# Storing the first 1664 rows of dw2 from GpSimd's queue by row number, eight of 128 partitions apart

## The chip, the cores and the metric

The kernel runs on one core of one Trainium2 chip. The core has five engines with a queue of instructions each: PE (TensorE, matrix multiply), DVE (VectorE), ACT (ScalarE), POOL (GpSimd) and SP (SyncE, here only for issuing transfers). Transfers between the chip's memory (DRAM) and the on-chip memory (SBUF, 128 partitions) can be issued by SP, ACT and POOL; sixteen transfer engines carry them out. A transfer adds 16 to its semaphore when it has landed, one for each transfer engine. The metric is the device time of one execution in microseconds (us), the median of the runs.

## The reference

What is computed is one backward step of a gated mix of two blocks, for one token: attention over a cache (32 heads, 4096 keys of 128) and a dense block with the mish activation (640 to 1728 to 640).

```python
def _fwd_reference(A_x, A_k_cache, A_v_cache, A_wq, A_wo, B_x, B_w1, B_b1, B_w2, gate_w):
    ...
    x = A_x
    g = _sigmoid((x * gate_w).sum(-1, keepdims=True))
    a = _A_ref(x, A_k_cache, A_v_cache, A_wq, A_wo)
    b = _B_ref(x, B_w1, B_b1, B_w2)
    return g * a + (1 - g) * b
...
    _out, _vjp = jax.vjp(_f, A_x, A_k_cache, A_v_cache, A_wq, A_wo, B_w1, B_b1, B_w2, gate_w)
    _grads = _vjp(grad_out)
    return (_out0, *[jnp.asarray(_g) for _g in _grads])
```

The outputs are the forward result and the gradients of all inputs but B_x. The gradients of the two caches have the size of the caches, 32 MB each; they are outer products of one row of numbers with one column per head. The gradient of w2, called dw2 here, is an outer product too: row f of its 1728 rows is the activation of f times one common row of 640 numbers.

## The kernel before

All in all 82 MB are read and 82 MB written. The kernel goes once over the 32 heads (loop variable h; `H - 1` rounds and a last one written out after the loop). For each head it loads K and V, transposes them in words of two bf16 on PE into PSUM (L515), copies them from there to SBUF with ACT (L524), multiplies them with q and with the gradient of the output (L538), takes the softmax and its backward step, makes the two outer products dv and dk on DVE (L598, two halves each) and stores them from SP (L616). Between these it works off two side jobs: the projections wq and wo in groups of four heads (g, `hh = h % 4`), and the dense block, cut into small steps in a list `mq`, of which each round takes some.

The order on every engine is the order of the program's text (a schedule by hand); an instruction waits for what it needs, and what stands behind it on its queue waits with it. SP's transfers use eight semaphores in turn, so an SP issue also waits until the transfer eight issues before has landed.

What matters here:

- `w2_sb` holds w2 in SBUF as 128 partitions of 13 rows of 640 (1664 rows), and the last 64 rows as a fourteenth slice on 64 partitions. Row `p * 13 + fc` of w2 stands on partition p in slice fc, so that each partition's 13 rows are 16,640 bytes in one piece in DRAM.
- When the dense block's sums are done, `m_dw2(fc)` (L501 to L503, ACT) writes slice fc of dw2 over slice fc of `w2_sb`. `dw2_some` takes the next one or two of them in a round, counted by `dw2_next`.
- In round `h == H - 4`, that is head 28 (L796 to L802), dw2 is stored: three pieces of the 1664 rows from SP (L799; slices 0 to 3, 4 to 7 and 8 to 12), the last 64 rows and the gradient of b1 from POOL (L800, L802). POOL has nothing else to do then and reaches its stores long before SP comes to head 28.
- In the same round, after the stores, ACT makes dwo of the group before with four instructions (`f_dwo`, L380), and SP stores it (L386).
- In round `h == H - 2` dw1 is stored (L805, L806).
- After the loop come the last head, the last group's wq and wo (L372, L383) with their stores, and the three small results, `fin_rows`, stored from POOL (L920 to L922). L948 stands for the closing instructions of the program.
- `dx_parts` is a float tile of which DVE fills one column per group; it is used from the second group on.
- `ident_bf` is the 128 x 128 identity, made by POOL at the start (L159, L160).

Of the kernel before, what the change touches and what calls it, by code (L numbers as in the profile page):

```python
# [8 lines left out]
ALU = mybir.AluOpType  # L9
AX = mybir.AxisListType  # L10
# [6 lines left out]
def kernel(  # L17
# [24 lines left out]
    nc = tc.nc  # L42
    P = 128
    _, H, Sk, Dh = A_k_cache.shape
# [8 lines left out]
    FR = F // P  # L53
    FM = FR * P
# [4 lines left out]
    W2P = [(0, 4), (4, 8), (8, FR)]  # L59
# [17 lines left out]
    dw2_v = out_8[0:FM, :].rearrange("(p fc) n -> p fc n", p=P)  # L77
# [11 lines left out]
    const = ctx.enter_context(tc.tile_pool(name="const", bufs=1))  # L89
# [59 lines left out]
    w2_sb = const.tile([P, FCN, D], BF16, name="w2_sb")  # L149
    for a, b in W2P:  # L150
# [7 lines left out]
    ident_bf = const.tile([P, P], BF16, name="ident_bf")  # L158
    nc.gpsimd.memset(ident_bf[:], 0.0)  # L159
    nc.gpsimd.affine_select(  # L160
        out=ident_bf[:], in_=ident_bf[:], compare_op=ALU.not_equal, fill=1.0,
        base=0, pattern=[[-1, P]], channel_multiplier=1,
# [20 lines left out]
    nc.vector.memset(aT_acc[:], 0.0)  # L183
    bT = const.tile([P, RC], F32, name="bT")
    dx_parts = const.tile([P, RC, NG + 3], F32, name="dx_parts")

    p4b, ds4b = [], []
    qz = const.tile([P, G, 2, 2, 16], BF16, name="qz")
# [57 lines left out]
    def g_qpair_cp(g):  # L246
        pair_cp(qz, groups[g].pop("pair"), 4)

    def g_docol(g):
        groups[g]["col"] = col_mm(groups[g]["do_row"])  # L250
# [163 lines left out]
    def m_np(fc):  # L414
        return P if fc < FR else FT
# [60 lines left out]
    def m_diag():  # L476
        nc.vector.tensor_copy(dh_bf[:, 0:FR], dh32[:, 0:FR])
        nc.vector.tensor_copy(dh_bf[0:FT, FR:FCN], dh32[0:FT, FR:FCN])
        nc.gpsimd.tensor_tensor(diag3, ident_bf[:].unsqueeze(2).to_broadcast([P, P, FR]),
                                dh_bf[:, 0:FR].unsqueeze(1).to_broadcast([P, P, FR]), ALU.mult)  # L480
        nc.gpsimd.tensor_tensor(mjunk[0:FT, FM:F], ident_bf[0:FT, 0:FT],
                                dh_bf[0:FT, FR:FCN].to_broadcast([FT, FT]), ALU.mult)
# [18 lines left out]
    def m_dw2(fc):  # L501
        n = m_np(fc)
        nc.scalar.activation(w2_sb[0:n, fc, :], db_bc[0:n, :], ACT.Copy, scale=act_f[0:n, fc:fc + 1])  # L503
# [14 lines left out]
    def ev():  # L518
        trq.pop(0)()
# [6 lines left out]
    def k_pe(h, c):  # L526
        if h < H:
            tr_pe(h, kts, KT, c)

    def v_pe(h, c):  # L530
        if h < H:
            tr_pe(h, vts, VT, c)
# [32 lines left out]
    def softmax(h):  # L565
        mx = s_ps.tile([P, P + 2], F32, name="mx", tag="mx")
        nc.tensor.transpose(mx[:, 0:P], dgms.pop(h)[:].to_broadcast([P, P]), ident_f[:])  # L567
        negM = small.tile([P, 1], F32, name="negM", tag="negM")
        nc.vector.tensor_reduce(negM[:], mx[:, 0:P], axis=AX.X, op=ALU.max, negate=True)  # L569
        return mx, negM  # L570

    def exps(h, negM):
        es[h] = small.tile([P, J], BF16, name="e_bf", tag="e_bf")
        zds[h] = small.tile([P, 2], F32, name="zd", tag="zd")
        nc.scalar.activation(es[h][:], sd[h][0], ACT.Exp, bias=negM[:], scale=scale, accum_out=zds[h][:, 0:1])  # L575
# [21 lines left out]
    def outer(dst, col4, row, a, b):  # L597
        nc.vector.tensor_tensor(  # L598
            dst[:, a:b, :].rearrange("p j (k t) -> p j k t", t=4),
            row.rearrange("p (k t) -> p k t", t=4).unsqueeze(1).to_broadcast([P, b - a, Dh // 4, 4]),  # L600
            col4[:, a:b, :].unsqueeze(2).to_broadcast([P, b - a, Dh // 4, 4]), ALU.mult)

    o_t = {}

    def out_half(w, h, dst, col4, row, k):
        hh = h % G
        if k == 0:
            if w == "k" and H - KBUFS <= h < H - 1:
                o_t[w, h] = kv_in.tile([P, J, Dh], BF16, name="Kn", tag="Kn")
            elif w == "v" and h > H - VBUFS:  # L610
                o_t[w, h] = kv_in.tile([P, J, Dh], BF16, name="Vn", tag="Vn", bufs=VBUFS)
            else:
                o_t[w, h] = outs.tile([P, J, Dh], BF16, name="o_sb", tag="o_sb")
        outer(o_t[w, h], col4, row[:, hh * Dh:(hh + 1) * Dh], k * JH, (k + 1) * JH)
        if k == 1:
            nc.sync.dma_start(dst[h], o_t.pop((w, h))[:])  # L616

    def dv_out(h, k):
        out_half("v", h, dVv, p4s[h], groups[h // G]["do_row"], k)
# [1 line left out]
    def dk_out(h, k):  # L621
        if h >= 0:
            out_half("k", h, dKv, ds4s[h], groups[h // G]["qs_row"], k)
# [12 lines left out]
    def dqo_red(h, x):  # L636
        if h >= 0:
            v = x[:].rearrange("p t r -> p (t r)")[:, 3:3 + 4 * (P - 1)].rearrange("p (s q) -> p s q", q=P - 1)
            nc.vector.tensor_reduce(groups[h // G]["dqo"][:, :, h % G],  # L639
                                    v[:, :, 0:P - 1:32].rearrange("p s (i c) -> p i s c", i=2),  # L640
                                    axis=AX.XY, op=ALU.add)
# [6 lines left out]
    m_cost = dict(h=0.8, b1=0.8, act=0.9, b=0.5, dh=0.9, diag=0.5, bc=0.5, dx=0.9, dw1=0.5, gap=0.0)  # L648
    m_fn = dict(h=m_h, b1=lambda i: (m_b1(), m_abs()), act=m_act, b=m_b, dh=m_dh,
                diag=lambda i: m_diag(), bc=m_bc, dx=m_dx, dw1=m_dw1)  # L650
    dw2_next = [0]

    def mlp_some(budget, pause=True):
        spent = 0.0
# [88 lines left out]
    for h in range(H - 1):  # L743
        g, hh = h // G, h % G
        nx, pv = g + 1 < NG, g > 0
        k_pe(h + 1, 2)
        ev()
        mx, negM = softmax(h)
        if hh == 3 and nx:
            g_qpair_cp(g + 1)  # L750
            g_docol(g + 1)
        dqo_red(h - 1, xs[h])
        k_pe(h + 1, 3)
        ev()
        exps(h, negM)
        dk_out(h - 1, 1)
        v_pe(h + 1, 0)
        if hh == 2 and nx:
            g_q(g + 1)
        v_pe(h + 1, 1)  # L760
        if hh == 3 and nx:
            g_dopair(g + 1)
            g_dopair_cp(g + 1)
        k_rows(h + 1)
        ev()
        ev()
        pjs(h)
        v_pe(h + 1, 2)
        ev()
        zd_mm(h, mx)  # L770
        if hh == 0 and pv:
            f_new(g - 1)
            f_diag(g - 1)
        elif h >= 2:
            mlp_some(0.9, False)
        v_pe(h + 1, 3)
        ev()
        probs(h, mx)
        if hh == 0 and pv:
            f_o4(g - 1)  # L780
            f_o4c(g - 1)
            f_bc(g - 1)
        dv_out(h, 0)
        k_pe(h + 2, 0)
        dq_o(h)
        v_rows(h + 1)
        rw_cp(h + 1)
        if h + 2 < H:
            ev()
        dv_out(h, 1)  # L790
        load_k(h + KBUFS)
        load_v(h + VBUFS)
        k_pe(h + 2, 1)
        if h + 2 < H:
            ev()
        if h == H - 4:  # L796
            assert dw2_next[0] == FCN
            for a, b in W2P:
                nc.sync.dma_start(dw2_v[:, a:b, :], w2_sb[:, a:b, :])  # L799
            nc.gpsimd.dma_start(out_8[FM:F, :], w2_sb[0:FT, FR, :])  # L800
            assert not any(k == "bc" for k, _ in mq)
            nc.gpsimd.dma_start(db1_row, dh_bc[0:1, :])  # L802
        if h == H - 2:
            assert not mq
            nc.sync.dma_start(dw1_v[:, 0:3, :], w1_sb[:, 0:3, :])  # L805
            nc.sync.dma_start(dw1_v[:, 3:RC, :], w1_sb[:, 3:RC, :])  # L806
        dk_out(h, 0)
        x_tr(h + 1)
        maxes(h + 1)
        if hh == 0:  # L810
            if nx:
                g_new(g + 1)
            if pv:
                l_pe(g - 1, 0, G)
                l_add(g - 1, g - 1, True)
                for t in range(G):
                    f_dwo(g - 1, t)
                f_dwo_st(g - 1)
                for c in range(2):
                    f_dx(g - 1, c)  # L820
                    f_dwq(g - 1, c)
        if hh == 1:
            if pv:
                for c in range(2, RC):
                    f_dx(g - 1, c)
                    f_dwq(g - 1, c)
                f_dwq_st(g - 1)
            if nx:
                w_pe("o", g + 1, 0)
                ev()  # L830
                w_pe("o", g + 1, 1)
                ev()
        if hh == 2:
            if g + 2 < NG:
                load_wo(g + 2)
            if not nx:
                for k in range(NWT):
                    w_pe("q", g, k)
                    ev()
            else:  # L840
                w_pe("o", g + 1, 2)
                ev()
                g_do(g + 1)
                g_qcol(g + 1)
                g_qpair(g + 1)
        if hh == 3:
            if g % 2 == 0 and g + 4 <= NG:
                load_wqp(g // 2 + 1)
            if nx:
                g_qs(g + 1)  # L850
        if h >= 2:
            mlp_some(0.9 if hh < 2 else 1.8)
            dw2_some(2)

    g, h = NG - 1, H - 1
# [97 lines left out]
```

## Time and profile before

| | us |
|---|---|
| median of 3 runs | 404.71 |
| lowest and highest of them | 404.71 to 405.26 |
| the profiled execution | 404.96 |
| its span, from the first instruction to the last | 403.18 |
| PE busy in the span | 305.9 |
| DVE busy | 287.9 |
| ACT busy | 232.4 |
| POOL busy | 11.8 |
| DRAM read and written, mean rate | 82.03 and 82.03 MB, 407 GB/s |

The page divides the span into 40 slices of 10.1 us; a digit is the busy share of an engine in that slice in tenths. Transfers are counted by queue: q1 is what SP issues, q0 what POOL issues, q8 and q14 fetch instructions. A group of instructions is named by its line, its engine, its operation and what it writes and reads. The windows view gives the busy time of each engine in chosen stretches, and behind it the granted clock of TensorE, the share of the sixteen transfer engines that was busy, and what they moved. The chain of waits is followed back from the last instruction, at each step to what released it. The sixteen increments of a transfer are read from the trace's record of semaphore updates by transfers.

### The profile page before, as it was taken

How to read it: one execution, taken by the hardware profiler on the slowest of the kernel's cores; microseconds unless marked ns; L12 is line 12 of the kernel's file. 1: busy time of each engine (PE TensorE's matmuls, PEld its weight loads, DVE VectorE, ACT ScalarE, POOL GpSimd, SP SyncE). 2: the span in 40 equal slices, each digit the busy share in tenths (PEclk: the TensorE clock that was granted, in tenths of full speed). 3: DMA queues.
4: the chain of work that ended last, by engine and by line, in shares of the span. 5: the costliest groups of instructions: out<-in, count | busy, mean ns of one | idle time of the engine just before them, and what ended most of it. 6: DMA issues, size and time to landing. Idle time of an engine off the chain costs nothing.

```text
span 403.2 us, 7688 instructions
## 1 busy us (share of the span) xinstructions
PE 305.9 (76%) x2930; PEld 207.0 (51%) x2945; DVE 287.9 (71%) x808; ACT 232.4 (58%) x468; POOL 11.8 (3%) x29
## 2 busy tenths in 40 slices
PE   2979989787897985876887779876886977677640
PEld 1556646464565663544555447544555645464420
DVE  2217738868678875769897956896997985679780
ACT  2466757754676563753668667765767655375220
POOL 3000001000000000000001200000000000000001
PEclk9999999988999998989998997988999899889555
DMA  7999999999999999999999999999999999999894
GB/s 274 428 416 423 417 424 415 417 423 424 422 422 426 423 414 424 424 418 428 422 423 428 424 418 424 427 418 423 422 419 424 425 417 425 426 422 377 360 389 153
DMA packets 28708, 164.55 MB, mean 408 GB/s; under 512 B 2991, under 2 KB 3056, under 8 KB 12288
## 3 DMA queue, kind: packets, MB, share of 16 engines
q1 hardware_dynamic: 28256, 163.97, 98.1%
q8 instruction: 23, 0.38, 0.4%
q0 software_dynamic: 384, 0.10, 0.1%
q14 instruction: 13, 0.11, 0.1%
q10 hardware_dynamic: 32, 0.01, 0.0%
HBM read 82.03 MB, written 82.03 MB: 407 GB/s over the span
## 4 chain that ended last, share of the span: by engine, by line
DMA 42%; PE 25%; DVE 22%; ACT 6%; issue 2%; POOL 0%; POOLq 0%; SPq 0%; DVEq 0%; ACTq 0%
DMA out_dram<-o_sb 40%; PE tr L515 9%; DVE o_sb L598 9%; PE rw L538 3%; PE rw L631 3%; DVE junk L362 3%; DMA wq_p<-in_A_wq_dram 2%; PE x L555 2%; DVE wq_p L372 2%; ACT rw_sb L549 2%; ACT do_row L266 2%; PE tr L324 2%; PE do_ps L263 1%; PE h_ps L405 1%; DVE mjunk L494 1%
## 5 line engine op out<-in xcount | busy, mean ns | idle before, releaser
L524 ACT COPY T<-tr 128x512 f32<-128x512 f32 x256 | 138.0, 595 | 53.0 <-PE tr L515 38.3
L598 DVE TENSOR_TENSOR o_sb<-qs_row,ds 128x2048 bf16<-128x2048 bf16 x58 | 70.8, 1220 | 37.6 <-DMA out_dram<-o_sb 37.5
L515 PE MATMUL tr<-ident_f,Kn 128*128 128x128 f32 x512 | 85.6, 295 | 5.8 <-DVE rw L508 5.8
L515 PE MATMUL tr<-ident_f,Vn 128*128 128x128 f32 x512 | 84.5, 299 | 6.6 <-ACT T L524 6.0
L515 PEld LDWEIGHTS tr<-ident_f,Vn 128*128 128x128 f32 x512 | 63.4, 154 | 27.3 <-PE tr L515 12.1
L515 PEld LDWEIGHTS tr<-ident_f,Kn 128*128 128x128 f32 x512 | 61.1, 149 | 23.2 <-PE rw L631 14.1
L598 DVE TENSOR_TENSOR o_sb<-do_row,p 128x2048 bf16<-128x2048 bf16 x58 | 68.2, 1218 | 0.0
L549 ACT COPY rw_sb<-rw 128x512 f32<-128x512 f32 x33 | 19.4, 587 | 51.2 <-PE rw L538 49.0
L631 PE MATMUL rw<-Kn,ds 128*4 128x512 bf16 x256 | 35.9, 405 | 6.4 <-DVE ds L593 5.7
L631 PE MATMUL rw<-Vn,p 128*4 128x512 bf16 x256 | 35.9, 405 | 0.0
L567 PE MATMUL mx<-ident_f,m_s 128*128 128x128 f32 x32 | 10.1, 316 | 29.7 <-DVE m_s L563 29.6
L555 PE MATMUL x<-ident_f,rw_sb 128*128 128x128 f32 x132 | 22.5, 295 | 4.4 <-ACT rw_sb L549 1.4
L362 DVE SCALAR_TENSOR_TENSOR junk<-wq_p,dq_bc 128x512 bf16<-128x512 bf16 x35 | 23.9, 684 | 0.0
L538 PE MATMUL rw<-T,qz 128*32 128x512 bf16 x256 | 22.3, 426 | 0.0
L575 ACT ACTIVATE e_bf<-x,negM 128x32 bf16<-128x32 f32 x32 | 9.3, 292 | 22.4 <-DVE dqo L639 22.1
L567 PEld LDWEIGHTS mx<-ident_f,m_s 128*128 128x128 f32 x32 | 4.5, 142 | 34.0 <-DVE m_s L563 33.9
L538 PE MATMUL rw<-T,doz 128*32 128x512 bf16 x256 | 21.4, 411 | 0.8 <-ACT T L524 0.8
L380 ACT ACTIVATE wo_g<-da_bc,o 128x640 bf16<-128x640 bf16 x28 | 20.9, 816 | 1.2 <-PE ax_ps L350 1.2
L583 PE MATMUL mx<-zd,ones_f 128*128 128x2 f32 x64 | 11.2, 245 | 13.5 <-DVE pj L579 13.4
L555 PEld LDWEIGHTS x<-ident_f,rw_sb 128*128 128x128 f32 x132 | 14.5, 145 | 13.2 <-ACT rw_sb L549 13.2
L569 DVE TENSOR_REDUCE negM<-mx 128x1 f32<-128x128 f32 x32 | 9.2, 288 | 16.1 <-PE mx L567 16.1
L631 PEld LDWEIGHTS <-ds 128*4 128x4 bf16 x256 | 9.1, 85 | 22.2 <-DVE ds L593 11.4
(174 smaller groups left out, 367.6 us busy)
## 6 DMA issues: line engine op xcount, KB each, us to landing
out_dram<-o_sb SPq DMA_DIRECT2D x58, 1024.0 KB, 16.6
Kn<-in_A_k_cache_dram SPq DMA_DIRECT2D x32, 1024.0 KB, 16.8
Vn<-in_A_v_cache_dram SPq DMA_DIRECT2D x32, 1024.0 KB, 17.3
wq_p<-in_A_wq_dram SPq DMA_DIRECT2D x4, 1280.0 KB, 8.7
wo_g<-in_A_wo_dram SPq DMA_DIRECT2D x8, 640.0 KB, 17.6
out_dram<-wo_g SPq DMA_DIRECT2D x8, 640.0 KB, 18.3
out_dram<-wq_p SPq DMA_DIRECT2D x4, 1280.0 KB, 16.3
out_dram<-Kn SPq DMA_DIRECT2D x3, 1024.0 KB, 11.4
```

The source lines that it names most:

```text
L362: nc.vector.scalar_tensor_tensor(jq[:], in0=wqs[g][:, c, :], scalar=1.0, in1=groups[g]["dq_bc"][:], op0=ALU.mult, op1=ALU.mult, accum_out= ...
L380: nc.scalar.activation(wos[g][:, hh, :], da_bc[:], ACT.Copy, scale=groups[g]["o4"][:, hh:hh + 1])
L515: nc.tensor.transpose(tp[:, t, :], words[:, t * P:(t + 1) * P], ident_f[:])
L524: nc.scalar.copy(T[h][:, (3 - c) * (TB // 2):(4 - c) * (TB // 2), :], tp[:])
L538: nc.tensor.matmul(rw[32 * c:32 * (c + 1), :], lhsT=z[:, par, :, :].rearrange("p m u -> p (m u)"), rhs=Tb[:, c, par, :, :], start=first an ...
L549: nc.scalar.copy(rw_sb[h][:].rearrange("p t r -> p (t r)"), rw[:])
L555: nc.tensor.transpose(xs[h][:, 3 - j, :], t[:, j, :], ident_f[:])
L567: nc.tensor.transpose(mx[:, 0:P], dgms.pop(h)[:].to_broadcast([P, P]), ident_f[:])
L575: nc.scalar.activation(es[h][:], sd[h][0], ACT.Exp, bias=negM[:], scale=scale, accum_out=zds[h][:, 0:1])
L583: nc.tensor.matmul(mx[:, P:P + 2], lhsT=ones_f[:], rhs=zds[h][:], start=True, stop=True)
L598: nc.vector.tensor_tensor(dst[:, a:b, :].rearrange("p j (k t) -> p j k t", t=4), row.rearrange("p (k t) -> p k t", t=4).unsqueeze(1).to_br ...
L631: nc.tensor.matmul(rw[32 * c:32 * c + 4, :], lhsT=c4[:, 4 * jb:4 * jb + 16].rearrange("p (j t) -> p t j", t=4)[:, 0, :], rhs=N[:, jb:jb + ...
```

## The change

The 1664 rows are no longer stored by SP. POOL stores them with an indirect transfer (a scatter): partition p goes to row `rowids[p]` of dw2 seen as 128 rows of 8320 numbers. The row number is p, except on partitions 16 to 19 and 48 to 51, where 4096 is added to it; these numbers are above the bound of 127, and their rows are left out. Two plain transfers of four partitions each, from POOL too, store them. The row numbers are made at the start, by an iota on POOL and seven small DVE instructions, with columns of `dx_parts` for scratch. Slice 0 of dw2 is no longer made with the others but in head 28, right before the stores (`dw2_next` begins at 1). The order on POOL in head 28 is then: the last 64 rows, the scatter, the two plain transfers, the gradient of b1. The line with `t = o_t.pop` is the same as before in two steps.

```diff
+    LATE = ((16, 20), (48, 52))
+    rowids = const.tile([P, 1], mybir.dt.int32, name="rowids")
+    scr = dx_parts[:].rearrange("p c k -> p (c k)")
+    nc.gpsimd.iota(rowids[:], pattern=[[0, 1]], base=0, channel_multiplier=1)
+    nc.vector.tensor_copy(scr[:, 0:1], rowids[:])
+    for i, (a, b) in enumerate(LATE):
+        nc.vector.reduce_sum(scr[:, 2 + i:3 + i], ident_bf[:, a:b], axis=AX.X)
+    nc.vector.tensor_tensor(scr[:, 2:3], scr[:, 2:3], scr[:, 3:4], ALU.add)
+    nc.vector.tensor_scalar(scr[:, 2:3], scr[:, 2:3], float(H * P), None, ALU.mult)
+    nc.vector.tensor_scalar(scr[:, 0:1], scr[:, 0:1], scr[:, 2:3], None, ALU.add)
+    nc.vector.tensor_copy(rowids[:], scr[:, 0:1])
+
+    def scat_st(rows, lim, dst, src):
+        ids = rowids[:].bitcast(mybir.dt.uint32)
+        nc.gpsimd.indirect_dma_start(out=rows, out_offset=bass.IndirectOffsetOnAxis(ap=ids, axis=0), in_=src,
+                                     in_offset=None, bounds_check=lim - 1, oob_is_err=False)
+        for a, b in LATE:
+            nc.gpsimd.dma_start(dst[a:b], src[a:b])
...
-    dw2_next = [0]
+    dw2_next = [1]
...
         if h == H - 4:
             assert dw2_next[0] == FCN
-            for a, b in W2P:
-                nc.sync.dma_start(dw2_v[:, a:b, :], w2_sb[:, a:b, :])
+            m_dw2(0)
             nc.gpsimd.dma_start(out_8[FM:F, :], w2_sb[0:FT, FR, :])
+            rows = out_8[0:FM, :].rearrange("(p fc) n -> p (fc n)", p=P)
+            scat_st(rows, P, rows, w2_sb[:, 0:FR, :].rearrange("p fc n -> p (fc n)"))
             assert not any(k == "bc" for k, _ in mq)
             nc.gpsimd.dma_start(db1_row, dh_bc[0:1, :])
```

More of the change, by code (lines that the diff above doesn't have):

```diff
@@ L615, in out_half @@
         if k == 1:
-            nc.sync.dma_start(dst[h], o_t.pop((w, h))[:])
+            t = o_t.pop((w, h))
+            nc.sync.dma_start(dst[h], t[:])
     def dv_out(h, k):
```

## The prediction

> **What bounds the kernel now.** I read the slices of the page first, then windows over the end, then the sixteen completion increments of each transfer, then the chain of waits, and last the rows of what the diff moves.
>
> ```profile
> DMA  7999999999999999999999999999999999999894
> GB/s 274 428 416 423 417 424 415 417 423 424 422 422 426 423 414 424 424 418 428 422 423 428 424 418 424 427 418 423 422 419 424 425 417 425 426 422 377 360 389 153
> ...
> q1 hardware_dynamic: 28256, 163.97, 98.1%
> ```
>
> The transfer engines are full from the second slice to the last three, nearly all through SP's queue (q1). No compute engine is over 76%. What is left to find is the end.
>
> ```profile
> core 0: us, PE busy (x) PEld busy (x) DVE busy (x) ACT busy (x) POOL busy (x), PEclk, DMA share, GB/s
> ...
> 391.00:396.00 5.00, 0.86 (x3) 0.59 (x3) 1.09 (x9) 0.26 (x1) 1.53 (x3) 0.50 1.00 389
> 396.00:397.50 1.50, 0.00 (x0) 0.00 (x0) 0.00 (x0) 0.00 (x0) 0.00 (x0) 0.50 0.48 171
> 397.50:398.50 1.00, 0.00 (x0) 0.00 (x0) 0.00 (x0) 0.00 (x0) 0.00 (x0) 0.50 0.06 23
> 398.50:402.20 3.70, 0.00 (x0) 0.00 (x0) 0.00 (x0) 0.00 (x0) 0.00 (x0) 0.50 0.06 23
> ```
>
> The last two numbers of a row are the share of the 16 transfer engines and GB/s. From 397.5 to 402.2 the share is 0.06, one sixteenth: **one transfer engine works alone for 4.7 us**, and nothing else does anything. The increments say the same. Every transfer adds 16 to its semaphore, one per engine. For the last store (wo_g, issued at 390.73) fourteen come at 396.94 to 397.10, one at 397.83, the last at 402.16. The distance from first to last grows all along: 0.5 us for the loads up to 28 us, 3.8 us for the K load issued at 119.2, 9.6 us for the store issued at 348.1. So one engine is slower than the others by some 2.5%. From 370 on the others wait for compute and it catches up to 5.2 us. It never idles from 367.24 on: its landings follow each other by 1.5 to 3.4 us, about each transfer's size.
>
> Nothing else sets the time before: the last landing, 402.16, plus 1.02 us of closing instructions is the span, 403.18. The profiled run took 404.96, the median of the runs is 404.71.
>
> **The change, part by part.**
>
> *Off the late engine.* The three dw2 pieces (5120 + 5120 + 6400 bytes a row, so 16,640 bytes for each of 128 rows, 8 rows an engine) land on it at 368.88, 370.50 and 372.45, the store ahead of them at 367.24: 5.21 us. A plain 8192-byte packet starts 306 ns after the one before, 26.8 bytes per ns, so 8 x 16,640 bytes cost at least 4.97. If the eight rows that the scatter leaves out are that engine's eight, it ends at 402.16 - 5.21 = 396.95.
>
> *The eight rows again.* Two transfers of four rows of 16,640 bytes: 0.62 us a row, so 2 x 0.62 = 1.24 us on each of four engines if both use the same four. The others idle: the share is 0.89 in 365 to 371 and 0.74 in 371 to 375, so (0.11 x 6 + 0.26 x 4) = 1.7 us each, and 0.4 us in 386 to 391. The 1.24 goes there. If that cover is gone, it is added to their end.
>
> *The other 120 rows* are the same bytes on the same 15 engines, from another queue, after 355.9. They fit where they were: without them these engines would be empty between about 362 and 372. POOL's row for 64 rows is 0.57 us, 5.5 to landing. No row shows an indirect transfer: bounds are 0.57 us and the 16 us until that gap closes; I take 1 to 3 us, near the plain row. Neither end costs anything; beyond 16 us it would push the 15 engines' end. Queued behind it on POOL are the two small transfers and db1 (no reader), then fin_rows 38 us later.
>
> *ACT.* The store now waits for m_dw2(0), which is moved from about 216 us to the middle of head 28:
>
> ```profile
> L503 ACT ACTIVATE w_sb<-db_bc,act_f x14: 809/821/852, 215.8 to 290.8; 128x640 bf16<-128x640 bf16 x13, 64x640 bf16<-64x640 bf16 x1
> ...
> L800 POOL DMA_DIRECT2D out_dram<-w_sb x1: 568/568/568, 291.9 to 291.9; - x1
> ```
>
> ```profile
> 353.96 1.08 ACT L524 COPY T<-tr 128x512 f32<-128x512 f32 x2
> ...
> 355.21 2.99 ACT L380 ACTIVATE wo_g<-da_bc,o 128x640 bf16<-128x640 bf16 x4 [0.17 <-PE ax_ps L350]
> ```
>
> ```profile
> 354.77 0.45 PE ax_ps L350 x19
> 355.23 2.98 ACT wo_g L380 x4
> 358.20 0.47 ACT T L524
> ...
> 393.67 0.53 POOL out_dram L920
> 394.20 0.51 POOL out_dram L921
> ```
>
> The first fence shows L503 at 0.82 us each and the POOL store that already follows it. The second is ACT in time: free at 355.04, wo_g at 355.21, with 0.17 us idle. The third is the chain of waits: wo_g stands on it, and from there it runs through PE, ACT and DVE without a DMA to fin_rows. So 0.82 - 0.17 = **0.65 us is added to all compute from 355 on**. Lower bound 0 (slack that the chain hides), upper 0.82. The 0.82 saved at 216 is worth nothing: there stores wait for transfers. Before, the 0.65 would also have cost nothing, since the late engine had 5 us queued; with that cover gone it counts.
>
> *SP.* Three issues (354.51 to 357.38) vanish; the next, wo_g at 358.23, waits for ACT anyway. SP's waits for the transfer eight issues back all ended earlier. 0.
>
> *Prologue.* Seven small DVE instructions and an iota. Nearest DVE rows are 0.15 to 0.29 us, so 1.1 to 2.0 us, between the memsets:
>
> ```profile
> 5.17 0.48 DVE L508 MEMSET rw<- 128x512 f32 x1
> 7.87 0.17 DVE L678 COPY cols_bf<-cols_ps 128x15 bf16<-128x15 bf16 x1 [2.22 <-PE cols_ps L676]
> ```
>
> DVE idles 2.22 us there for PE, which covers it. Were it not, the first store (issued at 33.96, while loads fill the engines to 40.4) still has 6 us. iota puts POOL's memsets back by some 0.3 us; they end at 4.6 and are first needed at 13.74. 0.
>
> *The new end.* SP's side: the late engine 396.95, the second-latest 397.83, the others 397.10 + 0.65 = 397.75; so 397.83 + 1.02 = 398.85. POOL's side is now later:
>
> ```profile
> L948 POOLq DRAIN  x3: 40/102/5555, 394.5 to 402.9; - x3
> ```
>
> This 5.56 us wait ended at 400.08, 0.54 after fin_rows' last increment (399.54, the late engine's). On fourteen engines fin_rows is in by 397.68. Plus 0.65 is 398.33, plus 0.54 is 398.87, plus the closing after SP's last wait (403.18 - 402.42 = 0.76) is **399.6 us of span**, 3.6 less. On 404.96 that is 401.4, on the median of the runs 401.1; I say 401.2. For this case alone: 400.3 (ACT's 0.65 hidden, 0.2 of chance) to 402.4 (plus 0.7 for an engine that gets fin_rows late, as the fifteenth's 398.35 did, and 0.5 if the four-row transfers fall on it).
>
> *The weak link is whose rows these are.* The trace does not name engines. It has one hint: each of the three fin_rows transfers has five packets of 256 bytes, and in each exactly one is late (at 397.99, 398.49, 398.99; the other twelve by 396.76). So five-row transfers use the same five engines each time, and the late one is among them. Eight rows are one engine's share, and four rows go to one engine fewer than five: that fits a late fifth. [...]
>
> **The rivals.**
>
> *No relief, about 404.7.* The scatter deals its rows out by another order, or the dropped rows still cost their engine its time, or what is slow is the memory behind these rows and not the engine. Then the late engine keeps its 5.21 us, ends near 402.2, and ACT's 0.65 hides behind it. For it: nothing in the trace shows an indirect transfer. Against the memory's share in it: packets of 1280 bytes of the 64-row load took 55 ns each, 52 apart, 24.6 bytes per ns, hardly below a full transfer's 26.8 though only half the rows were addressed. [...]
>
> *Slower: the late engine is among the four, 406.* Its place is the two small transfers. If the late engine is one that serves them and not the owner of the rows left out, it keeps its share and gets 1.24 us on top: 402.16 + 1.24 + 1.02 = 404.42, 1.24 more than now: 405.95. It decides from the first row put on that engine, as nothing idles there. For it: four of the five candidates serve four rows if the order is kept. Against it: the fit above.
>
> *Slower still: the scatter does not spread.* On eight engines 15 rows each are 9.3 us instead of 5.0; less 1.7 idle, 397.75 + 2.6 = 400.4, still a gain. On four engines 30 rows are 18.6 us: 397.75 + 13.6 - 1.7 = 409.7, a time of about 412. It turns into a loss from some 6 us more on any engine (402.16 - 397.75 + 1.7). The 64-row POOL store ran on all 16, which speaks against it.
>
> **How the numbers follow.** Relief as worked out 0.66, no relief 0.14, late engine among the four 0.12, no spread 0.08. About 0.2% (0.8 us) is what a measurement tells from no change. Faster 0.66 (the first), same 0.15 (the second and a bit), slower 0.19 (the last two, less the mild half of the last). The time is that of the first, 401.2. The range 400.2 to 405.3 takes in the first two, 0.80; the first one's own is 400.3 to 402.4.
>
> **What would show it.** Right: windows after about 397.9 have no stretch at share 0.06; wo_g's sixteen increments lie within 1 us or so; one L503 stands at 355.04 and wo_g at 355.9; q1 has 3 x 8 x 16 = 384 packets fewer; the last wait is POOL's, at about 398.9. Wrong: the 0.06 stretch stays (rival 1) or grows by 1.2 (rival 2); fin_rows' issue does not move (the 0.65 was hidden); or packets of the scatter after 374.

## The result, and the profile after

| | before | after |
|---|---|---|
| median | 404.71 us (404.52 to 405.33, 21 runs) | 405.25 us (404.97 to 406.78, 21 runs) |
| ratio to before, 95% interval | | 1.0016 (1.0009 to 1.0022) |
| profiled execution, its span | 404.96, 403.18 | 405.02, 403.2 |

The kernel got slower by 0.16%, some 0.6 us, where 3.5 us less was forecast. The page of the profile after, with the slices and the two transfer queues:

```profile
DMA  7999999999999999999999999999999999999796
GB/s 273 426 419 418 427 418 421 416 420 425 421 424 427 423 410 426 425 417 425 425 421 427 423 419 427 424 415 423 423 422 423 426 415 428 425 415 357 273 414 243
...
q1 hardware_dynamic: 27824, 161.83, 96.9%
q0 software_dynamic: 592, 2.23, 1.7%
```

The rows have moved from q1 to q0 as the diff says (2.13 MB). The slice that holds 373 to 383 us has fallen from 360 to 273 GB/s, and the last one has risen from 153 to 243: work was put off to the end. The windows view of after shows where:

```profile
core 0: us, PE busy (x) PEld busy (x) DVE busy (x) ACT busy (x) POOL busy (x), PEclk, DMA share, GB/s
...
375.00:378.00 3.00, 2.32 (x20) 2.06 (x17) 2.16 (x6) 0.71 (x2) 0.00 (x0) 0.50 0.08 22
...
396.00:397.50 1.50, 0.00 (x0) 0.00 (x0) 0.00 (x0) 0.00 (x0) 0.07 (x1) 0.50 1.05 399
397.50:398.50 1.00, 0.00 (x0) 0.00 (x0) 0.00 (x0) 0.00 (x0) 0.00 (x0) 0.50 1.03 400
398.50:402.20 3.70, 0.00 (x0) 0.00 (x0) 0.00 (x0) 0.00 (x0) 0.00 (x0) 0.50 0.22 81
```

The end looks wholly different: before, one engine worked alone from 397.5; now all sixteen are busy to 398.5 and a few beyond. The last store's increments (one from each transfer engine) tell it: ten come at 398.90 to 399.02 (before, fourteen at 396.94 to 397.10), the others 0.5, 1.3, 2.0, 2.5, 2.6 and 3.1 us later, at 402.0. The place where it was lost is 375 to 378: 22 GB/s there, where before had 350 GB/s at a share of 0.89:

```profile
375.00:378.00 3.00, 2.98 (x24) 2.92 (x25) 1.30 (x5) 0.71 (x2) 0.00 (x0) 0.50 0.89 350
```

(The view counts a packet where it starts. By the packets' own record some five engines are at work all that time, on long packets begun before.)

POOL in the timeline of after:

```profile
356.50 1.09 POOL L201 DMA_INDIRECT out_dram<-w_sb,rowids  x1 [64.96 <-ACT w_sb L522]
368.69 1.13 POOL L204 DMA_DIRECT2D out_dram<-w_sb  x2 [11.11 <-DMA out_dram<-w_sb,rowids]
```

The scatter is issued in 1.09 us and lands 11.9 us after its start. Only then do the two transfers of four rows start, since both write one tensor. Their eight packets of 16,640 bytes, from the trace's record of packets (start in us, ns taken):

```
369.94 3834    369.96 3980    370.02 2828    372.78 2065
373.66 4400    374.42 4078    374.81 3962    374.90 3671
```

The 120 packets of the same size in the scatter took 620 to 734 ns each. These eight take 28.8 us together in place of 5.0. While they run, one more engine is slow: its packets of 8192 bytes from SP's queue start at 375.26, 375.88, 376.49 and 377.10 and take 611 ns each, about twice the usual 309. By the landings it is the engine that comes last: of one store it runs eight such packets from 373.75 on, when the store ahead has just ended there (its last increment comes at 374.23), and they land at 378.04. While four engines are held so, SP's issues take longer too. SP's issues in the timeline before:

```profile
374.65 0.33 SPq L616 DMA_DIRECT2D out_dram<-Vn  x1
375.03 0.43 SPq L805 DMA_DIRECT2D out_dram<-w_sb  x1
375.51 0.99 SPq L806 DMA_DIRECT2D out_dram<-w_sb  x1
```

and after:

```profile
375.51 1.96 SPq L636 DMA_DIRECT2D out_dram<-Vn  x1
377.52 1.12 SPq L826 DMA_DIRECT2D out_dram<-w_sb  x1
378.69 1.27 SPq L827 DMA_DIRECT2D out_dram<-w_sb  x1
```

The three take 4.35 us in place of 1.75. The other engines ran empty meanwhile, and have the work left over at the end.

### The profile page after: what moved, and what is told of

Read it like the earlier page. It is cut to its first block, busy times and chain, and to the rows that moved or that the text cites. A ratio compares the mean times of both kernels' runs of the same rounds, so it can differ in the third digit from the quotient of the medians.

```text
span 403.2 us, 7714 instructions
## 1 busy us (share of the span) xinstructions
PE 310.6 (77%) x2945; PEld 211.6 (52%) x2945; DVE 288.5 (72%) x815; ACT 233.0 (58%) x468; POOL 14.2 (4%) x33
## 4 chain that ended last, share of the span: by engine, by line
DMA 41%; PE 25%; DVE 23%; ACT 7%; issue 2%; POOL 0%; POOLq 0%; SPq 0%; DVEq 0%; ACTq 0%
DMA out_dram<-o_sb 39%; PE tr L534 9%; DVE o_sb L617 9%; PE rw L557 3%; PE rw L651 3%; DVE junk L381 3%; DMA wq_p<-in_A_wq_dram 2%; PE x L574 2%; DVE wq_p L391 2%; PE tr L343 2%; ACT rw_sb L568 1%; ACT wo_g L399 1%; ACT do_row L285 1%; PE do_ps L282 1%; DVE junk L491 1%
## 5 line engine op out<-in xcount | busy, mean ns | idle before, releaser
L534 PE MATMUL tr<-ident_f,Vn 128*128 128x128 f32 x512 | 87.8, 308 | 8.6 <-ACT T L543 8.1
L534 PE MATMUL tr<-ident_f,Kn 128*128 128x128 f32 x512 | 86.7, 298 | 5.7 <-DVE dx_parts L194 5.7
L534 PEld LDWEIGHTS tr<-ident_f,Vn 128*128 128x128 f32 x512 | 66.8, 160 | 29.2 <-PE tr L534 12.1
L534 PEld LDWEIGHTS tr<-ident_f,Kn 128*128 128x128 f32 x512 | 62.0, 151 | 22.7 <-PE rw L651 13.7
```

The lines of the kernel that those rows point to most:

```text
L534: nc.tensor.transpose(tp[:, t, :], words[:, t * P:(t + 1) * P], ident_f[:])
```

## The experiments

The theory from this: what counts is the partitions read. The late engine and the four that serve the small transfers read the same eight partitions, and are slow because they read there together. The rivals: transfers of four long rows from POOL's queue are slow by themselves; the scatter brings no relief; something else that was added costs the time.

### The eight rows, not stored at all

```diff
-        for a, b in LATE:
-            nc.gpsimd.dma_start(dst[a:b], src[a:b])
```

> The two transfers of four rows are left out, so eight rows of dw2's first part are not stored at all (133 KB less). Theory (the scatter relieves the late engine; the whole of the gain is taken back by the eight packets of the two small transfers, which took 2.1 to 4.4 us each and blocked four engines): with them gone, SP's issues near 375.5 fall back from 1.96 to some 0.3 us, no stretch of four busy engines near 375 to 379, span near 399.6, time 401.2 (400.4 to 402.0), some 0.9% below before. Rival A (the scatter brings no relief at the end, or ACT's 0.65 us and what else moved costs as much): 404.4 to 405.3, as after. Rival B (the small transfers cost something, but half of the 5.2 us of relief is lost otherwise): 402.5 to 403.5.

402.21 us (401.79 to 402.34); ratio 0.9935 (0.9921 to 0.9948). The windows of this kernel:

```profile
375.00:378.00 3.00, 2.31 (x33) 1.69 (x25) 1.61 (x5) 1.30 (x3) 0.00 (x0) 0.88 0.80 319
...
396.00:397.50 1.50, 0.00 (x0) 0.00 (x0) 0.00 (x0) 0.00 (x0) 0.00 (x0) 0.50 0.32 113
397.50:398.50 1.00, 0.00 (x0) 0.00 (x0) 0.00 (x0) 0.00 (x0) 0.00 (x0) 0.50 0.00 0
```

The hole at 375 is gone, and the last store's sixteen increments lie within 1.3 us (396.70 to 398.02). So the relief came, and the whole of it was lost again in the two small transfers: they cost 405.25 - 402.21 = 3.0 us.

### Another engine's eight rows left out

```diff
-    LATE = ((16, 20), (48, 52))
+    LATE = ((20, 24), (52, 56))
...
-        for a, b in LATE:
-            nc.gpsimd.dma_start(dst[a:b], src[a:b])
```

> As the run without the small transfers, but the scatter leaves out rows 20 to 23 and 52 to 55 instead (these are not stored). Theory: one engine alone is late, and it is the one that serves rows 16 to 19 and 48 to 51; relieving its neighbour leaves it with its 5.2 us, a tail of one engine at the end as in before, time 404.7 to 405.2. Rival (what helps is that POOL's queue carries the rows, or that any engine has less to do): 401.2, as without the small transfers.

405.31 us (405.19 to 406.02); ratio 1.0016 (1.0007 to 1.0025). Its windows have the tail of before again:

```profile
397.50:398.50 1.00, 0.00 (x0) 0.00 (x0) 0.00 (x0) 0.00 (x0) 0.00 (x0) 0.50 0.15 56
398.50:402.20 3.70, 0.00 (x0) 0.00 (x0) 0.00 (x0) 0.00 (x0) 0.00 (x0) 0.50 0.06 24
```

In the store of wo_g that follows, one increment now comes 3.4 us ahead of all others (362.18), and the last one is late as ever (374.19). Eight rows are one engine's share, and the late engine's rows are 16 to 19 and 48 to 51.

### The small transfers from other partitions

First, the same two transfers to the same places in DRAM, from eight partitions spread out (eight rows then hold other rows' contents). If the partitions read are what counts, the time falls back near the 402.21 us without the small transfers:

```diff
-        for a, b in LATE:
-            nc.gpsimd.dma_start(dst[a:b], src[a:b])
+        for (a, b), c in zip(LATE, (3, 7)):
+            nc.gpsimd.dma_start(dst[a:b], src[c:c + 80:20])
```

> The two small transfers are kept, to the same eight rows of the output, but read partitions 3, 23, 43, 63 and 7, 27, 47, 67 in place of 16 to 19 and 48 to 51 (so eight rows hold other rows' contents). Bytes, packets, queue and places in DRAM are the same. [...] Rival (four rows of 16,640 bytes from POOL's queue, or their places in DRAM, are slow in themselves): packets still 2 to 4.4 us, time 405.3 as after.

402.12 us (401.96 to 402.65); ratio 0.9938 (0.9924 to 0.9951). The windows and SP's issue of this kernel:

```profile
375.00:378.00 3.00, 2.31 (x33) 1.68 (x25) 1.72 (x6) 1.20 (x3) 0.00 (x0) 0.85 0.80 319
...
397.50:398.50 1.00, 0.00 (x0) 0.00 (x0) 0.00 (x0) 0.00 (x0) 0.00 (x0) 0.50 0.02 5
```

```profile
375.07 0.33 SPq L636 DMA_DIRECT2D out_dram<-Vn  x1
```

The eight packets take 620 to 1259 ns, 6.6 us together. Bytes, queue and place in DRAM are those of after, and the time of issue is nearly the same (368.26, there 368.69); what was changed is the partitions read, and 3.1 us are won. Transfers of four long rows from POOL are not slow in themselves.

Then from the eight neighbours, which are another engine's share. If the late engine's rows alone are slow to read, the time is again near 402.1 us:

```diff
-            nc.gpsimd.dma_start(dst[a:b], src[a:b])
+            nc.gpsimd.dma_start(dst[a:b], src[a + 4:b + 4])
```

> As the kernel after, but the two small transfers read partitions 20 to 23 and 52 to 55, the neighbours (so eight rows of the output hold other rows' contents). [...]

403.87 us (402.95 to 405.45); ratio 0.9984 (0.9970 to 0.9998). The packets take 1266 to 4799 ns, 26.0 us together, and here too one engine's packets of 8192 bytes take 608 to 615 ns, six in a row from 373.28 on. So nothing is special about the late engine's rows: **in both sets tried, eight partitions that are one engine's share are slow to read for four other engines**. The time lies between, probably because the engine now slowed had slack and the late one has its relief; no run separates the two. The windows of this kernel:

```profile
371.00:375.00 4.00, 2.80 (x26) 1.39 (x30) 3.45 (x9) 1.76 (x4) 0.00 (x0) 0.78 0.90 265
375.00:378.00 3.00, 2.32 (x19) 1.59 (x12) 1.88 (x6) 0.59 (x1) 0.00 (x0) 0.50 0.64 249
```

Do eight such partitions give one engine's rate in all, however many engines read there? In after the slowed engine moves 8192 bytes in 611 ns, 13.4 bytes per ns, and beside it the second four long packets move 66,560 bytes between 373.66 and 378.77, 13.0 per ns. Together that is 26.4, and one engine alone has 26.8. So in this stretch the five have about one engine's rate together. (The trace does not name partitions: that this engine reads the same eight in SP's stores as it would in the scatter is inferred from its slowing beside these packets, 611 ns in place of 309.)

The first four long packets do not fit. They move 66,560 bytes between 369.94 and 374.84, 13.6 per ns, but the engine that is slowed later is not slowed then: the last increments of three stores, its own, come at 369.09, 371.65 and 374.23, so it moves 65,536 bytes in 2.6 us each time, some 25 per ns. That makes about 39 from the same eight partitions. So a fixed rate shared by all readers is not shown. What is shown is that four engines that read one other engine's eight partitions are slow together (all eight packets from first to last: 15 bytes per ns in after, 17 with the neighbours), and that this engine itself falls to half for part of that time. How the reads are shared stays open; whether four neighbouring partitions alone would do it was not tried either.

### The small transfers ahead of the scatter

```diff
     def scat_st(rows, lim, dst, src):
+        for a, b in LATE:
+            nc.gpsimd.dma_start(dst[a:b], src[a:b])
         ids = rowids[:].bitcast(mybir.dt.uint32)
...
-        for a, b in LATE:
-            nc.gpsimd.dma_start(dst[a:b], src[a:b])
```

> As the kernel after, but the two small transfers stand ahead of the scatter on POOL's queue, so that they start near 358 instead of 370 (the scatter then waits for them, as both write one tensor). [...] Rival (the bytes do no harm where the engines have time to make up for them, and only the place at 370 to 379 was bad): 401.5 to 402.8.

405.10 us (404.40 to 405.87); ratio 1.0007 (0.9997 to 1.0016). The packets take 2.6 to 4.6 us also here, 29.2 together, and the slowed engine's 611 ns, five in a row from 363.64 on and 624 once. The time alone decides nothing, though: the scatter now waits for the small transfers (it is issued at 368.96), SP's issue of the store at 360.13 takes 6.19 us, and the share of the sixteen engines is 0.31 from 362 to 367, which may cost something by itself.

### All 128 rows by the scatter

```diff
-    nc.vector.tensor_scalar(scr[:, 0:1], scr[:, 0:1], scr[:, 2:3], None, ALU.add)
+    nc.vector.tensor_scalar(scr[:, 2:3], scr[:, 0:1], scr[:, 2:3], None, ALU.add)
...
-        for a, b in LATE:
-            nc.gpsimd.dma_start(dst[a:b], src[a:b])
```

> The scatter stores all 128 rows and the small transfers are left out. The late engine keeps its 5.2 us, so the tail of before is back: all theories expect 404.7 to 405.3 if the queue alone changes nothing. It tells what the scatter and the moved ACT instruction cost by themselves: if they are hidden, 404.7 (within 0.2% of before); if the late engine loses more through POOL's queue, up to 405.5; if the scatter deals rows out by another order than a plain transfer (and the relief comes from that), near 401 to 402.

405.41 us (405.03 to 405.66); ratio 1.0015 (1.0006 to 1.0024). No relief, as the late engine has all its rows again (last landing 402.21). But it was also some 0.7 us slower than before, with its tail as before. This was not foreseen; the next kernels take it apart.

### Where 0.6 us come from that no wait shows

The row numbers alone, on top of before, at the start (the lines from `LATE` to `rowids` in the diff above):

> The kernel before plus the row numbers alone (iota and seven small DVE instructions at the start), no scatter and no move. It takes apart the 0.8 us by which the kernel with a scatter of all 128 rows was slower than before (405.41 against 404.6). If the start costs it: 405.0 to 405.4. If the scatter and POOL's queue, or the moved ACT instruction, cost it: 404.4 to 404.8, as before. The prediction had the start at nothing.

405.26 us (405.06 to 405.55); ratio 1.0015 (1.0006 to 1.0024). So it is in these lines. Made in the middle of the run, behind the last step of the activation (scratch in columns of `mt[0]`):

> The kernel before plus the row numbers alone, but made in the middle of the run (behind the last step of the activation, with a spare tile as scratch) and not at the start. The same nine instructions at the start cost 0.6 us (405.26 against 404.7). Theory (their place costs: at the start they delay a chain that everything hangs on): 404.5 to 404.8, as before. Rival (any such addition costs, by its place in memory or in the program): 405.1 to 405.4.

405.48 us; ratio 1.0020 (1.0011 to 1.0029). Their place in time is not it. Only the tile and the iota:

```diff
+    rowids = const.tile([P, 1], mybir.dt.int32, name="rowids")
+    nc.gpsimd.iota(rowids[:], pattern=[[0, 1]], base=0, channel_multiplier=1)
```

> The kernel before plus the iota alone at the start, on POOL, ahead of its memsets; no DVE instruction. If the eight small DVE instructions cost the 0.6 us, 404.5 to 404.8; if POOL's memsets coming later, or the one more tile, costs it, 405.1 to 405.4.

405.22 us; ratio 1.0013 (1.0004 to 1.0022). So it is not the DVE instructions either. The next three have no row numbers at all. The kernel before once more, with nothing but a remark added:

> The kernel before once more, with nothing changed but a remark behind its last line. If the 0.6 us of all small additions are a cost: 404.5 to 404.8. If they are how a second kernel stands to the first in such a comparison: 405.1 to 405.4, and the change itself is then no slower than before.

404.69 us; ratio 0.9998 (0.9989 to 1.0007). With POOL's memset of `h_sb` written twice:

> The kernel before with POOL's memset of h_sb done twice (0.11 us, at about 4.5 us, where POOL then idles for 9 us). If any added instruction costs 0.6 us by moving the program: 405.1 to 405.4. If the tile's place or the DVE instructions did: 404.5 to 404.8.

404.84 us; ratio 1.0002 (0.9993 to 1.0011). With a tile that nothing touches:

```diff
+    spare = const.tile([P, 1], F32, name="spare")
```

> The kernel before with one small tile more that nothing reads or writes, where the row numbers' tile stands, so that what is allocated behind it lies elsewhere. If the place in memory costs the 0.6 us: 405.1 to 405.4. If it is the instructions: 404.5 to 404.8.

405.31 us; ratio 1.0013 (1.0004 to 1.0022). **A tile of 4 bytes a partition, never used, costs 0.6 us.** What it does is move everything that is allocated behind it. Which part of that counts:

```diff
+    spare = const.tile([P, 1], F32, name="spare")
...
-    gg = const.tile([P, 1], F32, name="gg")
+    gg = spare[:, 0:1]
```

> The kernel before with the unused tile where the row numbers' stood, and another small tile of the same size (gg, behind it) taken away, gg being a part of the new one: the tiles between the two move, the K, V, output and weight pools behind them do not. If it is those pools' place that costs: 404.5 to 404.8. If it is the tiles between: 405.1 to 405.4.

404.78 us; ratio 1.0001 (0.9992 to 1.0010). The tiles between the two places move here, the pools behind do not, and nothing is lost: what costs is the place of what lies behind `gg`, the pools with the K, V, output and weight tiles above all. The traces do not show in what the loss consists: all of SP's packets together took 6.334 ms of engine time with the spare tile, and 6.330 and 6.333 in two executions of the kernel before. Why that place costs stays open.

The change itself, with the row numbers in a column of `mt[1]`, so that no tile is added:

```diff
-    rowids = const.tile([P, 1], mybir.dt.int32, name="rowids")
+    rowids = mt[1][:, 0:1].bitcast(mybir.dt.int32)
```

> The kernel after with the row numbers in a spare column of a tile that is there anyway, made in the middle of the run: the change itself without one more tile. [...] Rival (the change itself costs 0.6 us and the tile nothing here): 405.1 to 405.5.

404.75 us (404.46 to 405.48); ratio 1.0002 (0.9993 to 1.0011). Level with before: the long packets take 2.3 to 4.3 us here too, 28.3 together, so that what the scatter wins is lost in the small transfers again, and the 0.16% of after are the tile's.

### The eight partitions' rows from elsewhere

If the partitions read are what counts, these rows must be read from other partitions. A row of dw2 is one activation times a common row, so it can be made anywhere: the 104 activations are gathered onto partitions 0 to 103 by two small transfers, one ACT instruction makes the 104 rows of 640 in a tile that is free by then, and two plain transfers of 52 rows store them.

```diff
+    def lcol_ld():
+        for i, (a, b) in enumerate(LATE):
+            nc.gpsimd.dma_start(mt[0][i * LR:(i + 1) * LR, 0:1], act_f[a:b, 0:FR])
...
-        for a, b in LATE:
-            nc.gpsimd.dma_start(dst[a:b], src[a:b])
...
+                nc.scalar.activation(mjunk[0:2 * LR, 0:D], db_bc[0:2 * LR, :], ACT.Copy, scale=mt[0][0:2 * LR, 0:1])
...
+            for i, (a, b) in enumerate(LATE):
+                nc.gpsimd.dma_start(out_8[a * FR:b * FR, :], mjunk[i * LR:(i + 1) * LR, 0:D])
```

> All of the output is stored. The scatter stays as it is; the eight partitions' 104 rows of 640 (rows 208 to 259 and 624 to 675 of dw2) are made a second time on partitions 0 to 103 by one ACT instruction, from their 104 activations gathered by two small transfers, and stored from there by two plain transfers of 52 rows of 1280 bytes. [...] Rival (any second path for these rows costs what it wins, by POOL's queue or by the write order to one tensor): 404.5 to 405.5.

402.54 us (402.47 to 402.81); ratio 0.9949 (0.9935 to 0.9963). With the row numbers made in the middle of the run:

> The kernel with the 104 rows made elsewhere, with the row numbers made in the middle of the run. All of the output is stored. If the place of the nine instructions costs 0.6 us also where the late engine no longer sets the end: 401.9 to 402.1. If it cost only the late engine, or nothing there: 402.5, as before this move.

402.80 us; ratio 0.9952 (0.9939 to 0.9966). And that kernel without the added tile:

> The kernel with the 104 rows made elsewhere and the row numbers made in the middle (402.80 us), with the row numbers in a spare column of a tile that is there anyway, so that no tile is added and nothing moves in memory. All of the output is stored. If the added tile costs 0.6 us here too: 402.0 to 402.3. If it cost only the late engine's tail: 402.5 to 402.9.

**402.19 us (401.98 to 402.89); ratio 0.9942 (0.9928 to 0.9956)**, the fastest kernel that stores everything: 2.5 us less than before. Its last windows:

```profile
396.00:397.50 1.50, 0.00 (x0) 0.00 (x0) 0.00 (x0) 0.00 (x0) 0.00 (x0) 0.50 0.26 92
397.50:398.50 1.00, 0.00 (x0) 0.00 (x0) 0.00 (x0) 0.00 (x0) 0.00 (x0) 0.50 0.00 0
```

No engine works alone for long any more. The intervals of the last three overlap, so that here the tile's share (0.35 to 0.6 us by the medians) is likely, not shown.

## Why the prediction was wrong

The forecast was 401.2 us, and faster; the kernel took 405.25 and was no faster. The range of 400.2 to 405.3 takes this in, but only at its far end, which was put there for a late engine that keeps its rows. The late engine was relieved, so that end was met by another way, by luck.

- *What bounds the kernel, and whose rows these are*: right. Whose rows these are, no row of before shows; the runs do: with rows 16 to 19 and 48 to 51 left out the late engine's landings are some 5 us earlier (next point), and with the neighbour's eight left out it lands at 374.19 as before (374.12).
- *Off the late engine, 5.21 us*: right. The store of wo_g behind it lands last at 369.09 in place of 374.12, 5.03 us earlier.
- ***The eight rows again, 2 x 0.62 = 1.24 us on each of four engines*: the step that failed.** It took the row's price at an engine that reads alone. The four read the late engine's own eight partitions: 28.8 us for the eight packets in place of 5.0, so 7.2 on each of four engines if both transfers use the same four, with the late engine at half rate beside them for part of the time. The idle time of 1.7 us did not hold that, and SP's stalled issues carried it to the other engines. From 402.12 (read from other partitions) to 405.25 it cost 3.1 us.
- *No relief, the memory's share in it*: that rival looked for the fault in the memory behind these rows, and priced it at the wrong place. It was to leave the late engine late; in truth the late engine was relieved, and the delay came out on four others and SP. The argument against it, packets of 1280 bytes at nearly full rate (24.6 bytes per ns beside 26.8), was from a load, which writes to the on-chip memory; it does not show several engines reading the same eight partitions.
- *Prologue, 0*: the instructions cost nothing that could be measured (404.75 us with them and without the tile), but the tile that holds their result costs 0.6 us. No row of a profile shows that.
- *The other 120 rows*: right. The scatter is issued in 1.09 us, within the 1 to 3 taken, its packets take 0.62 us, and they land by 368.4. q1 has 432 packets fewer and not 384, as each of the three stores also had sixteen packets of 4 bytes. Not foreseen was that the small transfers wait 11.11 us for that landing.
- *ACT, 0.65 us*: its place was right (L522 stands at 355.34 for 0.85 us, wo_g behind it at 356.07 in place of 355.21). What it costs is not shown: from the row numbers alone (405.26) to the scatter of all rows (405.41) is 0.15 us, within the intervals, but there the late engine covers it. Nor can one profile tell: fin_rows is issued at 393.67 in the kernel before and at 392.31 in another execution of the same.
- *SP, 0*: wrong by 2.6 us of longer issues, but as a consequence of the held engines: with other partitions read, SP's issue at 375.07 takes 0.33 us again.
- *The new end, 399.6 us of span*: near where the slow reads are left out: 400.0 and 400.2 in the kernels without the small transfers and with other partitions, with the tile still in. fin_rows does land last there (398.63 and 398.74), but it was issued at 392.70 and 392.81, and not at 393.67 + 0.65 = 394.32; so that the forecast path gave so near a sum is in part luck.

So the forecast of 401.2 lacks 3.1 us for the slow reads and 0.6 for the tile; the 0.35 left are within the forecast's own range.

## What to carry to other kernels

A late transfer engine can be relieved, but in this case it paid only where the bytes taken from it were also read from other partitions, or not at all: four other engines that read the same eight partitions got 13 to 14 bytes per ns together where one alone has 26.8, SP's issue behind them rose from 0.33 to 1.96 us, and the other engines ran empty meanwhile. Where rows can be made again on other partitions for one cheap instruction, that is the better way: here 402.19 us in place of 404.75, both without the added tile. And before a loss of some tenths of a per cent is explained by an added instruction, add its tile alone.

## What the runs showed of the hardware beyond that

- A packet of 16,640 bytes that four engines read from one other engine's eight partitions takes 1.3 to 4.8 us in place of 0.62, and for part of that time most packets of that engine take 608 to 615 ns in place of 309, half the rate, in four kernels.
- While these engines were held, SP's issue of one transfer rose from 0.33 to 1.96 us, and another from 1.20 to 6.19 where the small transfers came first.
- An unused tile of 4 bytes a partition ahead of the large pools cost 0.13% (0.04 to 0.22), and nothing that could be measured (0.01%) where the pools stayed in place.
- Why one transfer engine falls behind by some 2.5% all along (9.6 us at the store issued at 348.1) is not found; taking eight rows from it only balances the end.
